# An attention and MLP kernel: the first chunk's squared scores stored unturned and turned where four later chunks read them

## Chip, cores and metric

The kernel runs on one core of one Trainium2 chip. The metric is the device time of one execution in microseconds (us). Every time below is of that kind or a time within one profiled execution.

## What is computed

For two samples (`batch` 2), with S = 3136 tokens, D = 256 features and 64 query features, the reference does three stages, one behind the other:

```python
scores = scale * np.matmul(z, z.transpose(0, 2, 1))   # scale = 1 / S
attn = np.maximum(scores, 0.0) ** 2
out = np.matmul(attn, v)
x = u * out
```

Then come `_moe_ref` (a rank 32 token mixing `x^T U V` and a channel MLP of 256 to 1024 to 256 with a ReLU) and `_moe2_ref` (the real part of an FFT over tokens and features, a normalisation and a second channel MLP). The change is in the first stage alone. Its matrix `attn` is symmetric, since queries and keys are both z.

## The kernel before, in words

**Tiles and steps.** Each sample b is cut into 7 chunks of CH = 448 queries; a chunk is written (b, qc). The keys are cut into 12 pairs of two times 128 keys, and a short pair 12 of 64 keys. One step is a chunk and a pair. A step makes a tile `A` of 128 x 896, keys on partitions, two halves of 448 queries in the row, with the squared scores, and splits it into a rounded high part `h` and the rest `l`. `values` then runs 24 matmuls with both (`psO`, line 780).

**Three ways to get `A`.** `scores` (lines 697 to 758) computes it: 6 matmuls on PE (`psS`, line 724), Relu and Square on ACT (lines 744 and 745), the cast to `h` on ACT or DVE (line 750 or 751, shown as L135 where ACT does it through the helper `hcopy`), and the subtraction `l` on DVE (helper `sub`, L138). Or the tile is a *kept* one: a chunk further back has already made these scores as seen from the other side, `keep` (lines 680 to 705) turned them on DVE in blocks of 32 x 32 (L690, L687 for pair 12) and stored them to DRAM (`kept_d`, L700, on the queues of POOL and SP), and `load_kept` (L671, on ACT's queue) reads them back; `split_kept` then only casts (ACT) and subtracts (DVE). What a chunk stores where is said by `_stored` and `_target`.

**What is kept.** `_kept` gives the pairs that chunk (b, qc) reads: all pairs that end before the chunk begins, but for sample 0 not the pairs 0 and 1, whose keys belong to the first chunk (pair 1 to the first and the second). The first chunk of sample 0 stores nothing. Pairs 0 and 1 of sample 0 have their keys in plain order (`_plain`): the first chunk of all takes its keys straight from its queries; everywhere else a pair's two halves are its even and its odd keys.

**What sets the order.** `_pairs` writes out the order of the 13 steps of each chunk: the steps of the kept pairs at given places, the others between them. The loop calls `ahead(i + 2)` and then `values(i)`, so scores or split of a step are issued two steps before its values. `ahead` also starts the load of a kept step three steps ahead (line 936), carries out the stores that the step before prepared, and drives background work: input loads, and converters of weights (L215 to L223 on DVE, L218 and L219 on ACT, tiles `stg`). PE, DVE, ACT and POOL carry out their instructions in the order in which they are issued; SP issues DMAs only.

**Buffers.** `P` (computed tiles) has 4, `h` and `l` have 3 each, `turned` (turned and loaded tiles) 5, `psS` 2.

Of the kernel before, what the change touches and what calls it, by code (L numbers as in the profile page):

```python
# [21 lines left out]
CH = 448  # L22
# [20 lines left out]

def _plain(b, p):
    return (b == 0) & (p < 2)


def _kept(b, qc):

    return [p for p in range(12) if 256 * (p + 1) <= qc * CH and (b or 256 * p >= CH)]  # L50

# [14 lines left out]
def _pairs(b, qc):  # L66

    plain = [*range(6), 12, *range(6, 12)]
    if qc == 0:
        return plain  # L70
    kept = _kept(b, qc)
    made = [p for p in range(12) if p not in kept]
    heavy = [p for p in made if _stored(b, qc, p)]
    bare = [p for p in made if p not in heavy]

    def merged(x, y):
        at = [((k + 0.5) / len(z), n, v) for n, z in enumerate((x, y)) for k, v in enumerate(z)]
        return [v for _, _, v in sorted(at)]

    places = sorted([12, 7, 8, 3, 10, 5, 4, 9, 2, 11][: len(kept)])  # L80
    short = 1 if len(kept) == 10 else 6
    places = [n for n in range(3, 13)] if short == 1 else places
    order = dict(zip(places, kept)) | {short: 12}
    rest = [n for n in range(13) if n not in order]
    order.update(zip(rest, bare[:2] + merged(bare[2:], heavy)))
    return [order[n] for n in range(13)]
# [38 lines left out]
def program(ctx, tc, zT, v, uT, U, V, w1a, w2a, w1b, w2b, b49, f64, fd, rep, mask, out):  # L125
# [28 lines left out]
    def run(gen):  # L154
# [13 lines left out]
        if _kept(b, c)  # L168
    }
    V_d = dram.tile([2 * RANK, S], F32R, tag="Vd", name="Vd")  # L170
    e_d = dram.tile([NB, 57 * 64], F32, tag="ed", name="ed")
# [316 lines left out]
    def attention(stack):  # L488
# [16 lines left out]
        def load_z(b, i, pairs=slice(0, 3)):  # L505

            raw = turned_tile()
            for j, r in enumerate(halves):
                if i < 4:
                    dma = late_dma if i == 0 or j and i > 1 else load  # L510
                    t0, n = 768 * i + 256 * pairs.start, pairs.stop - pairs.start
                    if _plain(b, 3 * i + pairs.start):
                        src = zT[b, :, t0 : t0 + 256 * n].rearrange("d (p j n) -> d j p n", j=2, n=128)
                        dma(out=raw[r, 0 : 128 * n].rearrange("d (p n) -> d p n", n=128), in_=src[:, j])
                    else:
                        dma(out=raw[r, 0 : 256 * n], in_=zT[b, :, t0 + j : t0 + j + 256 * n])
                else:
                    (late_dma if j else load)(out=raw[r, 0:64], in_=zT[b, :, S - 64 : S])
            zraw[b, i] = raw
# [24 lines left out]
        def split_z(b, i, pairs=slice(0, 3)):  # L544
# [3 lines left out]
            if i < 4:  # L548
                h, l = (KT[b][:, 3 * i : 3 * i + 3, k][:, pairs] for k in range(2))
                n = pairs.stop - pairs.start  # L550
                if _plain(b, 3 * i + pairs.start):
                    raw = raw[:, 0 : 128 * n].rearrange("d (p n) -> d p n", n=128)
                else:
                    raw = raw[:, 0 : 256 * n].rearrange("d (p n w) -> d p n w", n=128, w=2)[:, :, :, 0]
                (nc.vector.tensor_copy if (b, pairs.start) == (0, 2) else hcopy)(h, raw)
                sub(l, raw, f(h))
                return
# [28 lines left out]
        def load_v(b, p):  # L586
# [5 lines left out]
            if p < 12:  # L592
                how = "(a p) n -> p a n" if _plain(b, p) else "(p a) n -> p a n"
                load(out=raw, in_=v[b, p * 256 : p * 256 + 256, :].rearrange(how, a=2))
            else:
# [67 lines left out]

        prob, kept, loads, writes, turns = {}, {}, [None, None], [], []

        def load_kept(b, qc, p):
            own = next((k for k in range(2) if loads[k] not in kept), None)
            A = kept[b, qc, p] = ptile() if own is None else turned_tile()
            if own is not None:
                loads[own] = b, qc, p  # L670
            nc.scalar.dma_start(out=c2(A), in_=kept_d[b, qc][256 * p : 256 * p + 256].rearrange("(m j) n -> m j n", j=2))  # L671

# [8 lines left out]
        def keep():  # L681
# [13 lines left out]
            def write():  # L695
                for k, (a, to, col) in enumerate(_stored(b, qc, p)):
                    t0, t1 = max(rows.start, 0 if b else 512), min(rows.stop, 256 * (to * CH // 256))
                    m0, m1 = (n * (x - rows.start) // 32 for x in (t0, t1))
# [5 lines left out]

            writes.append(write)

        def scores(b, qc, p):
# [5 lines left out]
            for kk, kq in ((0, 0), (0, 1), (1, 0)):  # L713
                for j, r in enumerate(halves):
                    if p == 12:
                        k = KTl[b][r, kk]
                    elif (b, qc) == (0, 0) and p < 2:
                        c = 256 * p + 128 * j
                        k = q[r, kk, c : c + 128]
                    else:  # L720
# [4 lines left out]
                    elif (kk, kq) == (0, 0):  # L725
                        dst = extra if j else ps[:, j]
                        mm(dst[:, 0:w], first_q[r, c : c + 128], first_q[r, 0:w], start=True, stop=True)
            A, h, l = ptile(), ctile("h", F32R), ctile("l", F32R)
# [13 lines left out]
            else:  # L742
# [13 lines left out]
                if stored:  # L756
                    turns.append((b, qc, p, A))
            prob[b, qc, p] = (h, l)

# [165 lines left out]
        def ahead(i):  # L925
            if i < len(steps):
# [7 lines left out]
                elif i:  # L934
                    scores(b, qc, p)
                if i + 3 < len(steps) and steps[i + 3][2] in _kept(*steps[i + 3][0:2]):
                    load_kept(*steps[i + 3])
                for write in done:
# [484 lines left out]
```

## Time and profile before

| what | value |
|---|---|
| median of 3 runs | 1084.86 us (1084.63 to 1085.54) |
| the profiled execution's own time | 1084.36 us |
| span of that execution in the trace | 1082.6 us |
| granted clock of TensorE (1.00 is full speed) | 1.00 |
| PE, DVE, ACT, POOL busy, share of the span | 99%, 78%, 58%, 24% |
| chunk (0,2), first to last values | 82.90 to 119.88 us |
| chunk (0,3) | 119.88 to 155.26 us |
| chunk (0,4) | 155.26 to 189.27 us |
| chunk (0,5) | 189.27 to 222.92 us |

A chunk's stretch goes from the first matmul of its values to the first of the next chunk's. PE is the matmul engine, PEld its weight loads, DVE the vector engine, ACT the scalar engine, SP and POOL the engines whose queues carry most DMAs. The views used are the page's parts, the groups of instructions by line and shape, the engines by stretch, the chain of waits, and the timelines of one engine. In the view by stretch below, the five rows are the chunks (0,2) to (0,5) and the chunk (1,2) of the other sample; behind each engine's busy time stands its count of instructions in brackets.

### The profile page before, as it was taken

The numbers are of one execution on the slowest core, as the hardware profiler recorded it, in microseconds if no ns is written. First come the engines' busy times: TensorE is split into PE (matmuls) and PEld (weight loads), VectorE is DVE, ScalarE is ACT, GpSimd is POOL, SyncE is SP. The second block draws the span as 40 slices with busy tenths as digits, with TensorE's granted clock in tenths as the row PEclk, the third lists the DMA queues.
The fourth block names the chain that finished last, engine by engine and source line by source line (L and its number), as shares of the span: only waits on it lengthen the run. The fifth ranks groups of instructions, "written<-read, shape, count | busy, mean of one in ns | idle before, by whom it ended". The sixth has DMA issues, their size and how long they took to land.

```text
span 1082.6 us, 21193 instructions
## 1 busy us (share of the span) xinstructions
PE 1075.2 (99%) x7926; PEld 1005.4 (93%) x7926; DVE 848.0 (78%) x1571; ACT 623.8 (58%) x1094; POOL 255.5 (24%) x426
## 2 busy tenths in 40 slices
PE   9999999999999999999999999999999999999998
PEld 7999999999999999989899999999999999999997
DVE  7898888988998988656667876676687888778863
ACT  7888777768888877543333534343355454444431
POOL 2133345222343344121101121211131111011100
PEclk9999999999999999999999999999999999999999
DMA  6256567784666677785532553321253221121210
GB/s 178 78 145 174 162 190 223 231 273 117 185 193 195 192 239 221 264 259 175 156 89 71 155 158 101 79 75 40 66 132 96 61 91 44 35 67 45 60 43 35
DMA packets 140519, 146.04 MB, mean 135 GB/s; under 512 B 72534, under 2 KB 113530, under 8 KB 140416
## 3 DMA queue, kind: packets, MB, share of 16 engines
q1 hardware_dynamic: 108704, 70.57, 22.7%
q0 software_dynamic: 23280, 47.72, 15.3%
q10 hardware_dynamic: 8432, 26.40, 7.6%
q8 instruction: 62, 1.02, 0.4%
q14 instruction: 41, 0.34, 0.1%
HBM read 88.61 MB, written 56.00 MB: 134 GB/s over the span
## 4 chain that ended last, share of the span: by engine, by line
PE 95%; ACT 2%; DMA 1%; DVE 1%; issue 0%; SPq 0%; ACTq 0%; DVEq 0%
PE psO L780 37%; PE psC L460 8%; PE psC L459 8%; PE psC L458 8%; PE psH L435 8%; PE psH L433 8%; PE psH L434 8%; PE psS L724 6%; DMA scr<-wst 0%; ACT P L744 0%; DMA vraw<-in_v 0%; PE ps_m L1183 0%; ACT P L745 0%; PE ps_g L1183 0%; PE ps_x L1183 0%
## 5 line engine op out<-in xcount | busy, mean ns | idle before, releaser
L780 PE MATMUL psO<-h,Vt 64*128 64x448 f32 x2744 | 321.3, 360 | 0.5 <-DVE h L751 0.2
L780 PEld LDWEIGHTS psO<-h,Vt 64*128 64x128 f32 x2744 | 267.8, 184 | 16.3 <-DVE h L751 1.9
L438 ACT ACTIVATE Hh<-psH 128x448 fp32r<-128x448 f32 x224 | 121.4, 543 | 245.0 <-PE psH L435 243.6
L439 DVE SCALAR_TENSOR_TENSOR Hl<-psH,Hh 128x448 fp32r<-128x448 f32 x224 | 138.1, 619 | 111.0 <-ACT Hh L438 109.1
L138 DVE TENSOR_TENSOR l<-P,h 128x896 fp32r<-128x896 f32 (+2 forms) x188 | 170.6, 914 | 50.1 <-ACT h L135 43.2
L780 PE MATMUL psO<-l,Vt 64*128 64x448 f32 x1372 | 183.2, 359 | 0.1
L433 PE MATMUL psH<-h,w 128*128 128x448 f32 x448 | 165.1, 368 | 0.0
L435 PE MATMUL psH<-h,w 128*128 128x448 f32 x448 | 162.6, 363 | 0.0
L460 PE MATMUL psC<-Hh,w 128*128 128x448 f32 x448 | 162.5, 363 | 0.0
L434 PE MATMUL psH<-l,w 128*128 128x448 f32 x448 | 162.4, 363 | 0.0
L459 PE MATMUL psC<-Hl,w 128*128 128x448 f32 x448 | 162.3, 362 | 0.0
L458 PE MATMUL psC<-Hh,w 128*128 128x448 f32 x448 | 162.1, 362 | 0.0
L700 POOL DMA_DIRECT2D kept<-turned x178 | 112.9, 640 | 155.6 <-DVE turned L690 106.7
L780 PEld LDWEIGHTS psO<-l,Vt 64*128 64x128 f32 x1372 | 138.5, 184 | 7.8 <-DVE l L138 1.0
L744 ACT ACTIVATE P<-psS 128x896 f32<-128x896 f32 (+1 forms) x124 | 107.9, 870 | 22.7 <-PE psS L724 21.3
L745 ACT ACTIVATE P<-P 128x896 f32<-128x896 f32 (+1 forms) x124 | 113.1, 912 | 3.9
L135 ACT CAST h<-P 128x448 fp32r<-128x448 f32 (+1 forms) x111 | 80.2, 733 | 57.7 <-DVE P L324 39.6
L433 PEld LDWEIGHTS psH<-h,w 128*128 128x128 f32 x448 | 84.2, 188 | 6.3 <-issue 0.3
L459 PEld LDWEIGHTS psC<-Hl,w 128*128 128x128 f32 x448 | 84.0, 188 | 6.2 <-DVE Hl L439 0.4
L434 PEld LDWEIGHTS psH<-l,w 128*128 128x128 f32 x448 | 84.2, 188 | 5.6
L458 PEld LDWEIGHTS psC<-Hh,w 128*128 128x128 f32 x448 | 84.0, 188 | 5.9 <-issue 0.2
L460 PEld LDWEIGHTS psC<-Hh,w 128*128 128x128 f32 x448 | 84.1, 188 | 5.3
(299 smaller groups left out, 1359.3 us busy)
## 6 DMA issues: line engine op xcount, KB each, us to landing
turned<-kept ACTq DMA_DIRECT2D x49, 448.0 KB, 4.0
kept<-turned POOLq DMA_DIRECT2D x102, 112.0 KB, 3.6
uT<-in_uT SPq DMA_DIRECT2D x14, 448.0 KB, 5.7
out<-P SPq DMA_DIRECT2D x27, 224.0 KB, 1.9
aTd<-turned POOLq DMA_DIRECT2D x13, 448.0 KB, 4.1
kept<-turned SPq DMA_DIRECT2D x51, 112.0 KB, 2.9
aNd<-turned POOLq DMA_DIRECT2D x40, 112.0 KB, 3.7
scr<-wst SPq DMA_DIRECT2D x16, 256.0 KB, 2.0
```

What stands on the lines that cost most here:

```text
L138: tt(out=o, in0=a, in1=b, op=ALU.subtract)
L433: mm(ps[:, 0:CH], wh, self.h[:, a], start=a == 0, stop=False)
L434: mm(ps[:, 0:CH], wh, self.l[:, a], start=False, stop=False)
L435: mm(ps[:, 0:CH], wl, self.h[:, a], start=False, stop=a == 1)
L438: act(out=h, in_=ps[:, 0:CH], func=AF.Relu)
L439: stt(out=l, in0=ps[:, 0:CH], scalar=0.0, in1=f(h), op0=ALU.max, op1=ALU.subtract)
L458: mm(dst, wh, h, start=k == 0, stop=False)
L459: mm(dst, wh, l, start=False, stop=False)
L460: mm(dst, wl, h, start=False, stop=k == 7)
L700: (load if k % 2 and qc < 3 else late_dma)(out=kept_d[b, to][t0:t1, col : col + n].rearrange("(b r) k -> r b k", r=32), in_=t[quads[a], m0 ...
L745: act(out=A[:, x], in_=A[:, x], func=AF.Square)
L780: mm(o[fa][i][:, 0:CH], vt[r, j, k, fa * 128 : fa * 128 + 128], x[r, j * CH : j * CH + CH], start=n0 == 0 and fa not in [t[1][0] for t in ...
```

## The change

Chunk (0,0) writes the squared scores of pairs 3 to 10 to a DRAM tile `first_d` as they are, eight writes of 448 KB on POOL's queue. The chunks (0,2) to (0,5) (`LATE`) now have pairs 0 and 1 among their kept ones. Their tiles are read on SP's queue, four steps ahead: for pair 0 four pieces of 32 partitions from `first_d`, for pair 1 three pieces from `first_d` and one, already turned, from `kept_d`. One step before the split, `turn_read` turns the pieces on DVE (L692 of the new file) into a `P` tile. The plain layout goes away; the first chunk now takes every other query as keys. The stored rows for those chunks begin at 448 in place of 512. `_pairs` sets new places:

| chunk | pairs in order, before | pairs in order, after |
|---|---|---|
| (0,2) | 0 1 5 6 3 7 12 8 9 4 10 11 2 | 3 4 5 6 7 0 12 8 1 9 10 11 2 |
| (0,3) | 0 1 7 5 8 9 12 2 3 10 6 11 4 | 5 6 7 2 8 9 12 0 3 10 1 11 4 |
| (0,4) | 0 1 8 2 9 7 12 3 4 10 5 11 6 | 7 8 9 2 3 0 12 4 1 10 5 11 6 |
| (0,5) | 0 1 8 2 10 3 12 4 5 9 6 11 7 | 8 9 10 2 3 0 12 4 1 5 6 11 7 |

Kept before were pair 2 in (0,2), pairs 2 to 4 in (0,3), 2 to 6 in (0,4) and 2 to 7 in (0,5); pairs 0 and 1 join them. The core of the diff:

```diff
+LATE = (2, 3, 4, 5)
+
+def _unturned(b, qc, p):
+    return b == 0 and qc in LATE and p < 2
...
-    return [p for p in range(12) if 256 * (p + 1) <= qc * CH and (b or 256 * p >= CH)]
+    return [p for p in range(12) if 256 * (p + 1) <= qc * CH and (b or 256 * p >= CH or qc in LATE)]
...
     places = sorted([12, 7, 8, 3, 10, 5, 4, 9, 2, 11][: len(kept)])
+    if _unturned(b, qc, 0):
+        others, at = kept[2:], {3: (0, 1), 5: (1, 3)}.get(len(kept), (2, 4))
+        for p, k in enumerate(at):
+            others.insert(k, p)
+        places = [5, 8, 12] if len(kept) == 3 else places
+        kept = others
...
+    first_d = dram.tile([S, CH], F32, tag="firstd", name="firstd")
...
-            nc.scalar.dma_start(out=c2(A), in_=kept_d[b, qc][256 * p : 256 * p + 256].rearrange("(m j) n -> m j n", j=2))
+            rows = slice(256 * p, 256 * p + 256)
+            if not _unturned(b, qc, p):
+                nc.scalar.dma_start(out=c2(A), in_=kept_d[b, qc][rows].rearrange("(m j) n -> m j n", j=2))
+                return
+            n = (CH - rows.start) // 64 if p else 4
+            src = first_d[qc * CH : qc * CH + CH, rows.start : rows.start + 64 * n].rearrange("(b s) (q c) -> q s b c", s=32, c=64)
+            for q in range(n):
+                load(out=A[quads[q]].rearrange("s (b c) -> s b c", c=64), in_=src[q])
+            B = None
+            if n < 4:
+                B = ptile()
+                load(
+                    out=c2(B)[quads[3]], in_=kept_d[b, qc][rows][64 * n :].rearrange("(m j) n -> m j n", j=2)
+                )
+            unturned[b, qc, p] = B, slice(0, 32 * n)
+
+        def turn_read(b, qc, p):
+            B, r = unturned.pop((b, qc, p))
+            B = ptile() if B is None else B
+            nc.vector.transpose(
+                out=B[r].rearrange("p (j b s) -> p j b s", j=2, s=32),
+                in_=kept[b, qc, p][r].rearrange("p (b c j) -> p j b c", j=2, c=32),
+            )
+            kept[b, qc, p] = B
...
                     elif (b, qc) == (0, 0) and p < 2:
-                        c = 256 * p + 128 * j
-                        k = q[r, kk, c : c + 128]
+                        k = dealt(q[r, kk, 256 * p : 256 * p + 256], j)
...
+                if b + qc == 0 and 256 * (p + 1) > LATE[0] * CH and 256 * p < (LATE[-1] + 1) * CH:
+                    dst = first_d[256 * p : 256 * p + 256].rearrange("(m j) n -> m j n", j=2)
+                    writes.append(lambda: late_dma(out=dst, in_=c2(A)))
...
-                if i + 3 < len(steps) and steps[i + 3][2] in _kept(*steps[i + 3][0:2]):
-                    load_kept(*steps[i + 3])
+                for s in steps[i + 3 : i + 5]:
+                    if s[2] in _kept(*s[0:2]) and _unturned(*s) == (s != steps[i + 3]):
+                        load_kept(*s)
+                if steps[i + 1 : i + 2] and steps[i + 1] in unturned:
+                    turn_read(*steps[i + 1])
```

Line numbers of the new file: `hcopy` L144, `sub` L147, the converters L225 to L233, the new turn L692, `keep` L715 and L712, Relu and Square L771 and L772, DVE's cast L778. Where instructions stand now is shown at three places.

DVE in chunk (0,2), from the `keep` turn behind step 3 on; steps 4 to 7 (pairs 3, 7, 12, 8 before; 7, 0, 12, 8 now). Before:

```order
L690 STREAM_TRANSPOSE turned<-P 128x14x2x32
L751 CAST h<-P 128x896
L138 TENSOR_TENSOR l<-P,h 128x896 x2
L215 TENSOR_SCALAR stg<-stg 128x192
L216 TENSOR_SCALAR stg<-stg 128x192
L138 TENSOR_TENSOR l<-P,h 64x448
L690 STREAM_TRANSPOSE turned<-P 128x14x2x32
L687 STREAM_TRANSPOSE turned<-P 64x448
L751 CAST h<-P 128x896
L138 TENSOR_TENSOR l<-P,h 128x896
```

Now:

```order
L715 STREAM_TRANSPOSE turned<-P 128x14x2x32
L147 TENSOR_TENSOR l<-P,h 128x896
L692 STREAM_TRANSPOSE P<-turned 128x896
L147 TENSOR_TENSOR l<-P,h 128x896
L715 STREAM_TRANSPOSE turned<-P 128x14x2x32
L225 TENSOR_SCALAR stg<-stg 128x192
L226 TENSOR_SCALAR stg<-stg 128x192
L147 TENSOR_TENSOR l<-P,h 64x448
L712 STREAM_TRANSPOSE turned<-P 64x448
L778 CAST h<-P 128x896
L147 TENSOR_TENSOR l<-P,h 128x896
L692 STREAM_TRANSPOSE P<-turned 96x896
```

The cast of step 4 has gone to ACT, the turn of step 5 (L692) stands in front of that step's subtraction, and a second turn, of step 8, stands behind the subtraction of step 7.

ACT in chunk (0,2), from the Relu of step 7 to the Square or cast of step 9; `Us` is a converter's output. Before:

```order
L744 ACTIVATE P<-psS 128x896
L745 ACTIVATE P<-P 128x896
L744 ACTIVATE P<-psS 128x896
L745 ACTIVATE P<-P 128x896
L135 CAST h<-P 128x896
L135 CAST Q<-qraw 128x448
L135 COPY Us<-stg 128x192
L744 ACTIVATE P<-psS 128x896
L745 ACTIVATE P<-P 128x896
L671 DMA turned<-kept_76 128x896
```

Now:

```order
L771 ACTIVATE P<-psS 128x896
L772 ACTIVATE P<-P 128x896
L144 CAST h<-P 128x896
L144 CAST Q<-qraw 128x448
L144 COPY Us<-stg 128x192
L771 ACTIVATE P<-psS 128x896
L772 ACTIVATE P<-P 128x896
L144 CAST h<-P 128x896
```

Step 8 is now a cast alone, of the tile that DVE turned, ahead of the Q cast, the copy and the Relu of step 9.

DVE in chunk (0,4), from the subtraction of pair 12 (step 6) on; steps 7 and 8 are pairs 3 and 4 before, 4 and 1 now. Before:

```order
L138 TENSOR_TENSOR l<-P,h 64x448
L138 TENSOR_TENSOR l<-turned,h 128x896
L687 STREAM_TRANSPOSE turned<-P 64x448
L221 SCALAR_TENSOR_TENSOR stg<-stg 128x196
L222 SCALAR_TENSOR_TENSOR stg<-stg 128x196
L223 TENSOR_TENSOR stg<-stg 128x196
L138 TENSOR_TENSOR l<-turned,h 128x896
```

Now:

```order
L147 TENSOR_TENSOR l<-P,h 64x448
L147 TENSOR_TENSOR l<-turned,h 128x896
L712 STREAM_TRANSPOSE turned<-P 64x448
L692 STREAM_TRANSPOSE P<-turned 96x896
L231 SCALAR_TENSOR_TENSOR stg<-stg 128x196
L232 SCALAR_TENSOR_TENSOR stg<-stg 128x196
L233 TENSOR_TENSOR stg<-stg 128x196
L147 TENSOR_TENSOR l<-P,h 128x896
```

The new turn of pair 1 stands between the turn of pair 12 for `keep` and a converter's three steps, ahead of the subtraction of step 8.

## Rows read from the trace of the kernel before

**Rows 1.** The page, part 1, busy time, share of the span, instructions of each engine.
```profile
PE 1075.2 (99%) x7926; PEld 1005.4 (93%) x7926; DVE 848.0 (78%) x1571; ACT 623.8 (58%) x1094; POOL 255.5 (24%) x426
```

**Rows 2.** The page, part 4, the chain that ended last, shares by engine.
```profile
PE 95%; ACT 2%; DMA 1%; DVE 1%; issue 0%; SPq 0%; ACTq 0%; DVEq 0%
```

**Rows 3.** Stretch, length, busy PE PEld DVE ACT POOL, clock, DMA share, GB/s.
```profile
82.90:119.88 36.98, 36.86 (x368) 33.86 (x366) 32.26 (x47) 30.04 (x41) 11.84 (x18) 1.00 0.57 158
119.88:155.26 35.38, 35.38 (x356) 32.80 (x354) 30.27 (x49) 27.49 (x40) 18.08 (x29) 1.00 0.64 188
155.26:189.27 34.01, 34.01 (x344) 32.35 (x342) 29.45 (x49) 27.61 (x41) 15.58 (x25) 1.00 0.74 218
189.27:222.92 33.65, 33.65 (x340) 32.67 (x338) 29.88 (x50) 25.11 (x40) 8.37 (x13) 1.00 0.69 223
328.85:364.30 35.45, 35.45 (x359) 34.79 (x356) 32.55 (x49) 30.18 (x42) 11.57 (x18) 1.00 0.71 198
```

**Rows 4.** The chain of waits inside (0,4): start, length, what.
```profile
171.98 0.60 PE psS L724 x6
172.58 4.80 PE psO L780 x48
```

**Rows 5.** Groups by line and shape, DVE, 82.9 to 222.92 us, the four chunks.
```profile
L138 DVE TENSOR_TENSOR l<-P,h 128x896 fp32r<-128x896 f32 x33 | 36.0, 1092 | 8.2 <-ACT h L135 6.4
L690 DVE STREAM_TRANSPOSE turned<-P 128x896 f32<-128x896 f32 x18 | 19.9, 1104 | 0.1
...
L751 DVE CAST h<-P 128x896 fp32r<-128x896 f32 x21 | 13.0, 619 | 2.3 <-ACT P L745 2.3
```

**Rows 6.** The same view, ACT.
```profile
L745 ACT ACTIVATE P<-P 128x896 f32<-128x896 f32 x33 | 31.5, 955 | 1.0
L744 ACT ACTIVATE P<-psS 128x896 f32<-128x896 f32 x34 | 31.0, 912 | 4.8 <-PE psS L724 4.4
...
L135 ACT CAST h<-P 128x896 fp32r<-128x896 f32 x12 | 11.3, 945 | 0.4
```

**Rows 7.** The timeline of DVE in (0,2), start, length, instruction.
```profile
92.86 1.11 DVE L690 STREAM_TRANSPOSE turned<-P 128x896 f32<-128x896 f32 x1
...
101.55 0.35 DVE L221 SCALAR_TENSOR_TENSOR stg<-stg 128x192 int32<-128x192 int32 x1
...
102.49 1.11 DVE L690 STREAM_TRANSPOSE turned<-P 128x896 f32<-128x896 f32 x1
```

**Rows 8.** The timeline of DVE in (0,4).
```profile
171.40 1.09 DVE L138 TENSOR_TENSOR l<-turned,h 128x896 fp32r<-128x896 f32 x1 [0.51 <-PE psO L780]
172.41 0.63 DVE L687 STREAM_TRANSPOSE turned<-P 64x448 f32<-64x448 f32 x1
```

**Rows 9.** The timeline of ACT in (0,2).
```profile
90.47 0.95 ACT L745 ACTIVATE P<-P 128x896 f32<-128x896 f32 x1
...
102.81 0.94 ACT L135 CAST h<-P 128x896 fp32r<-128x896 f32 x1
...
104.38 0.91 ACT L744 ACTIVATE P<-psS 128x896 f32<-128x896 f32 x1
...
106.18 0.44 ACT L218 ACTIVATE stg<-stg,maskc 128x192 int32<-128x192 uint16 x1
...
106.87 0.90 ACT L744 ACTIVATE P<-psS 128x896 f32<-128x896 f32 x1
```

**Rows 10.** The timeline of PE in (0,2).
```profile
101.87 1.76 PE L780 MATMUL psO<-h,Vt 64*128 64x448 f32 x16
...
113.37 1.07 PE L780 MATMUL psO<-h,Vt 64*128 64x448 f32 x8
```

**Rows 11.** The timeline of ACT in (0,4).
```profile
172.11 0.56 ACT L135 CAST Q<-qraw 128x448 fp32r<-128x448 f32 x1
...
174.25 0.91 ACT L744 ACTIVATE P<-psS 128x896 f32<-128x896 f32 x1
...
176.18 0.95 ACT L135 CAST h<-P 128x896 fp32r<-128x896 f32 x1
```

**Rows 12.** The timeline of PE in (0,4).
```profile
177.82 1.77 PE L780 MATMUL psO<-h,Vt 64*128 64x448 f32 x16
```

**Rows 13.** DMA issues of the whole run: count, KB each, median us to landing.
```profile
turned<-kept ACTq DMA_DIRECT2D x49, 448.0 KB, 4.0
...
kept<-turned SPq DMA_DIRECT2D x51, 112.0 KB, 2.9
```

More of the change, by code (lines that the diff above doesn't have):

```diff
@@ L41, in _orders @@
     return o1, o2, c1, c2, tok, feat
-def _plain(b, p):
-    return (b == 0) & (p < 2)
+LATE = (2, 3, 4, 5)
+def _unturned(b, qc, p):
+    return b == 0 and qc in LATE and p < 2
 def _kept(b, qc):
-    return [p for p in range(12) if 256 * (p + 1) <= qc * CH and (b or 256 * p >= CH)]
+    return [p for p in range(12) if 256 * (p + 1) <= qc * CH and (b or 256 * p >= CH or qc in LATE)]
 def _target(p, a):
@@ L511, in load_z @@
                     t0, n = 768 * i + 256 * pairs.start, pairs.stop - pairs.start
[L512 to L516, printed above, removed]
+                    dma(out=raw[r, 0 : 256 * n], in_=zT[b, :, t0 + j : t0 + j + 256 * n])
                 else:
@@ L550, in split_z @@
                 n = pairs.stop - pairs.start
[L551 to L554, printed above, removed]
+                raw = raw[:, 0 : 256 * n].rearrange("d (p n w) -> d p n w", n=128, w=2)[:, :, :, 0]
                 (nc.vector.tensor_copy if (b, pairs.start) == (0, 2) else hcopy)(h, raw)
@@ L592, in load_v @@
             if p < 12:
-                how = "(a p) n -> p a n" if _plain(b, p) else "(p a) n -> p a n"
-                load(out=raw, in_=v[b, p * 256 : p * 256 + 256, :].rearrange(how, a=2))
+                load(out=raw, in_=v[b, p * 256 : p * 256 + 256, :].rearrange("(p a) n -> p a n", a=2))
             else:
@@ L662, in conversions @@
                 yield conv_w(w2a, k, True, wa[1])
-        prob, kept, loads, writes, turns = {}, {}, [None, None], [], []
+        prob, kept, loads, writes, turns, unturned = {}, {}, [None, None], [], [], {}
         def load_kept(b, qc, p):
@@ L696, in write @@
                 for k, (a, to, col) in enumerate(_stored(b, qc, p)):
-                    t0, t1 = max(rows.start, 0 if b else 512), min(rows.stop, 256 * (to * CH // 256))
+                    t0, t1 = max(rows.start, 0 if b else CH if to in LATE else 512), min(rows.stop, 256 * (to * CH // 256))
                     m0, m1 = (n * (x - rows.start) // 32 for x in (t0, t1))
@@ L705, in keep, with dealt @@
             writes.append(write)
+        def dealt(x, j):
+            return x.rearrange("d (n w) -> d n w", w=2)[:, :, j]
         def scores(b, qc, p):
@@ L726, in scores @@
                         dst = extra if j else ps[:, j]
-                        mm(dst[:, 0:w], first_q[r, c : c + 128], first_q[r, 0:w], start=True, stop=True)
+                        mm(dst[:, 0:w], dealt(first_q[r, 0:256], j), first_q[r, 0:w], start=True, stop=True)
             A, h, l = ptile(), ctile("h", F32R), ctile("l", F32R)
```

## Prediction

> **What bounds the kernel now.** The page's first line is read first: the matmul engine PE is busy 99% of the span, DVE 78%, ACT 58% [rows 1]. The chain that ended last is 95% PE [rows 2]. So a matmul that goes away is worth its full time, unless something else then makes PE wait. Next the stretches of the four chunks that change, (0,2) to (0,5): PE is busy 36.86 of 36.98 us in (0,2) and all of the time in the others, but DVE is busy 32.26, 30.27, 29.45 and 29.88 us, 87%, 86%, 87% and 89% of its stretches, far above its mean over the kernel, and ACT 75% to 81% [rows 3]. Both take their instructions in order, so a wait on either passes to all that stands behind it. What a step costs PE is seen in the chain of a stretch: 0.60 us for six score matmuls, 4.80 us for two steps of values, 2.40 each [rows 4].
>
> **What the change removes.** Eight score steps (pairs 0 and 1 in four chunks): 8 x 0.60 = 4.8 us of PE. This is the gain if no wait appears. ACT loses a Relu of 0.912 and a Square of 0.955 per step [rows 6]; of the casts some move from DVE (0.619 [rows 5]) to ACT (0.945 [rows 6]), as a kept step is always cast on ACT. ACT so gains at least 0.92 us per step.
>
> **What it adds on DVE.** A turn of 128x896 per step, priced by the turn of the same shape that `keep` makes: 1.104 us [rows 5]. Where a DVE cast of 0.619 goes, the net is 0.49; eight times that is 3.9 us, in chunks where DVE has only 3.8 to 5.1 us of idle time each [rows 3]. That alone fits. What counts is the place: the turn stands on DVE behind the subtraction of the step before (and often behind a `keep` turn), and ACT's cast of the turned step stands in front of the next Relu in ACT's queue. Before, ACT started such a step from PSUM alone. Now ACT must wait for DVE, and the next computed step waits behind that.
>
> **The walk through (0,2).** Step n's values are v(n). Pair 0 is step 5, pair 1 step 8. On DVE a `keep` turn starts at 92.86 [rows 7]. Behind it stand the subtraction of step 4 (1.09, its successor 1.0 later, as 171.40 to 172.41 [rows 8]), then the new turn (1.03 the same way): it ends near 96.0. ACT has finished step 4's Square at 91.42 [rows 9], casts until 92.4 and then stands until 96.0. Its cast of step 5 ends near 96.95. On DVE follow subtraction and `keep` (2.05), the converters' two short steps; ACT, with its own two converter steps (0.7, as 106.18 to 106.87 [rows 9]) in between, reaches Relu of step 7 only near 100.05, its Square ends near 101.95, and DVE's cast (0.6) at 102.5. PE began v(7) at 101.87 [rows 10] and is now ready 1.2 earlier, at 100.67: it waits about 1.85. Then subtraction, second turn and cast of step 8 end at 105.6, where PE is ready at 105.5: 0.1. Behind that cast stand the Q cast and a copy, so Relu of step 9 starts near 106.3 instead of 104.38 [rows 9]. ACT had no idle time from 102.81 on in this stretch, and has none now: Relu, Square and cast of step 9 end at 109.1 (PE ready 108.6, wait 0.5), those of step 10 at 112.6 (ready 111.5, wait 1.1), and DVE's cast of step 11, behind a conversion (0.94, as 101.55 to 102.49 [rows 7]) and a `keep`, at 116.25 (ready 115.6, wait 0.65). v(11) began at 113.37 [rows 10]. The waits are 4.2, less 1.2 for two score steps: **+3.0 us**.
>
> **The walk through (0,4).** Pair 1 is step 8, right behind pair 12, step 6. The subtraction of step 7 began at 171.40 [rows 8]; DVE has a turn in place of a cast ahead of it (+0.49), and 0.51 idle there; I take half, 171.65. Then `keep` of pair 12 (from 172.65, 0.56), then the new turn, 173.2 to 174.3. ACT's cast of step 8 then runs from 174.3 to 175.25; before, the Q cast behind it began at 172.11 [rows 11]. Q, key and converter casts (about 1.1) follow, and Relu of step 9 starts at 176.3 instead of 174.25, 2.05 later. Its cast began at 176.18 and ended at 177.13 [rows 11]; now it ends near 179.2. v(9) began at 177.82 [rows 12] and cannot start before 179.2, so the chunk loses **1.4 us**, though PE could be ready at 177.82 - 1.2 = 176.6.
>
> **The other two.** In (0,3) the turned steps are 7 and 10, with computed steps 9 and 11 behind them as in (0,4): I take the same **+1.4**. In (0,5) the step after the second turned one is a kept one, so the casts on ACT delay no Relu: the last wait of (0,4), by which PE ready at 178.3 behind a v(8) that starts at 175.3 stands until 179.2, falls away. 1.4 - 0.9 = **+0.5**. Sum: 3.0 + 1.4 + 1.4 + 0.5 = +6.3 us.
>
> **Loads, writes and layout.** The reads from the first chunk's scores go on SP, in 112 KB pieces of 256-byte rows, four per step, four steps ahead; the turn is one step ahead, so at least 3 x 2.40 = 7.2 us remain. The nearest row is the write of the same size and row length on the same queue, 2.9 us to landing, and a 448 KB read of long rows takes 4.0 [rows 13]. Bounds: 2.9 if the four overlap, 11.6 if they follow one another. I take 4 to 5, nearest the 448 KB read, so hidden: nothing. On SP input loads queue behind them; they are issued steps ahead too. The Trainium skill, "DMA: Bandwidth & Descriptors", section "Specifications", speaks against such rows: it asks for at least 512 bytes for line rate, and says that below this the engine reads, modifies and writes. By it the estimate would be twice the long-row read, 8.0 us, so 0.8 late where the lead is 7.2; the write's 2.9 us for rows of 256 bytes speaks against that as far as writes show it. The eight 448 KB writes of the first chunk go on POOL behind no one's critical load but the late keys of that chunk: nothing, at most half of a 4.0 us transfer, 2.0, if keys come late. The strided weight loads of the first chunk are 14; with a mean load of 1005.4/7926 = 0.127 us [rows 1], a doubling in plain sight would be 1.8; I take nothing, as PE hides loads under the matmul before. V of pairs 0 and 1 now comes in one longer row: nothing, or a gain of some tenths.
>
> **Sum.** The profiled execution took 1084.36 us; the median of the runs is 1084.86, 0.5 above it. 1084.36 + 6.3 + 0.5 = 1091.2 us.
>
> **Rivals.** *The waits are absorbed, faster.* Sample 1's chunks have the same number of kept steps, already turned; (1,2) takes 35.45 us with DVE busy 92% and PE 100% [rows 3], 1.53 less than (0,2). So a full DVE alone does not stop PE. If the turns land in DVE's gaps, or PE's queue is further ahead than I reckon, the kernel gets the 4.8: 1084.36 - 4.8 + 0.5 = 1080.1, up to 1082.5 with 2.4 of waits left. It decides for this when waits sum to less than 2.6 us of the 11.1 I find. Against it: in (0,2) Relu of step 9 has no ACT idle time behind it to be caught up in. Chance 0.27. *Gain and waits cancel*, each wait about half of what I walked: 5.6 less 4.8 is +0.8, 1085.7, and 1082.5 to 1087 around it. Chance 0.12. *The SP reads come late*, because they follow one another on the queue or stand behind a stalled input load: DVE, in order, then stands at the turn with all its work. Landing 0.8 us after DVE gets there, at each of the eight places, adds 6.4 to the forecast: 1097.6. Chance 0.08; it is outside the range. By the Trainium skill's rule above, this would be the case to expect. *The change does not do what it says*: that PE makes the eight steps anyway is excluded by its order, which drops 48 matmuls; no chance of its own.
>
> **How the numbers follow.** My forecast, waits of the size walked, has 0.53 and its own range 1087 to 1094: the lower end two thirds of the waits (7.4 - 4.8 + 1084.86), the upper one the walk plus the 2.0 of late keys and some tenths. Its place is 1091.2. The range 1080.1 to 1094.0 takes in both other cases and leaves out the late reads and the edges. About 0.2% (2.2 us) is what a measurement of this kernel can tell from no change: faster by more 0.27, within 0.12, slower by more 0.08 + 0.53 = 0.61.
>
> **What would show it.** Right: PE busy less by about 4.8 us but the span longer; in (0,2) and (0,4) the chain leaves PE for DVE turns and ACT casts; ACT idle time before casts of turned steps, ended by the new DVE turn; (0,2) near 40 us, (0,5) near 34. Wrong: chunks shorter by 1.2 us each with PE 99% busy or more in them (waits absorbed), or DVE idle before the new turns, ended by a DMA of the first chunk's scores (late reads), or the first chunk longer (layout or late keys).

## The result and the profile after

The changed kernel takes 1092.14 us (median of 6 runs, 1091.07 to 1094.77), the kernel before 1085.05 us beside it (1084.50 to 1085.63). The ratio is 1.0068 with an interval of 1.0055 to 1.0081: slower by about 7.1 us, where 1091.2 us, slower by 6.3, was forecast.

Two lines of the changed kernel's page (span 1091.3 us): busy time of each engine, and the chain's shares by engine.

```profile
PE 1075.1 (99%) x7878; PEld 1001.6 (92%) x7878; DVE 851.2 (78%) x1571; ACT 616.1 (56%) x1086; POOL 260.9 (24%) x434
...
PE 88%; ACT 4%; DVE 3%; DMA 3%; issue 2%; SPq 1%; ACTq 0%; DVEq 0%; POOL 0%
```

PE makes 48 matmuls fewer than before (7878 against 7926 [rows 1]), the eight score steps. Yet its busy time has not changed, 1075.1 against 1075.2 us. The chain, 95% PE before [rows 2], is now 88% PE, with ACT 4% and DVE 3%.

The four chunks of the changed kernel by stretch, from the first values of the chunk to those of the next; columns as in [rows 3].

```profile
82.91:122.92 40.01, 37.09 (x357) 33.10 (x354) 33.34 (x47) 28.09 (x39) 11.57 (x18) 1.00 0.65 177
122.92:161.01 38.09, 35.35 (x344) 31.38 (x342) 31.07 (x49) 25.74 (x38) 17.11 (x28) 1.00 0.70 196
161.01:196.53 35.52, 34.37 (x332) 30.38 (x330) 30.44 (x49) 25.78 (x39) 15.87 (x26) 1.00 0.77 226
196.53:231.73 35.20, 33.07 (x326) 30.99 (x325) 30.54 (x50) 23.25 (x38) 8.01 (x13) 1.00 0.77 238
```

| chunk | before, us | after, us | measured | forecast |
|---|---|---|---|---|
| (0,2) | 36.98 | 40.01 | +3.03 | +3.0 |
| (0,3) | 35.38 | 38.09 | +2.71 | +1.4 |
| (0,4) | 34.01 | 35.52 | +1.51 | +1.4 |
| (0,5) | 33.65 | 35.20 | +1.55 | +0.5 |
| sum | 140.02 | 148.82 | +8.80 | +6.3 |

The span is 8.7 us longer (1091.3 against 1082.6), so all of the loss lies in these four chunks. The profiled execution took 1093.06 us, 0.9 above its kernel's median, and that of before 0.7 below; the medians differ by 7.1. Since 4.8 us of score matmuls went away, the four chunks hold 8.80 + 4.8 = 13.6 us of new waits.

Where PE waits in (0,2) of the changed kernel: the first matmul rows of v(3), v(7), v(9), v(10) and v(11), with PE's idle time before each and what ended it.

```profile
91.82 1.88 PE L810 MATMUL psO<-h,Vt 64*128 64x448 f32 x16 [0.34 <-DVE h L778]
...
102.63 1.87 PE L810 MATMUL psO<-h,Vt 64*128 64x448 f32 x16 [1.16 <-DVE h L778]
...
109.36 1.87 PE L810 MATMUL psO<-h,Vt 64*128 64x448 f32 x16 [0.21 <-ACT h L144]
...
112.82 1.88 PE L810 MATMUL psO<-h,Vt 64*128 64x448 f32 x16 [0.78 <-ACT h L144]
...
116.41 0.88 PE L810 MATMUL psO<-h,Vt 64*128 64x448 f32 x6 [0.30 <-DVE h L778]
```

Before, v(7) and v(11) began at 101.87 and 113.37 [rows 10]. What holds PE is the high part `h`, cast on ACT or DVE. ACT's timeline in the same stretch, its casts of the two turned steps (5 and 8) and the Relu of step 9:

```profile
96.07 0.94 ACT L144 CAST h<-P 128x896 fp32r<-128x896 f32 x1 [3.65 <-DVE P L692]
...
104.87 0.94 ACT L144 CAST h<-P 128x896 fp32r<-128x896 f32 x1 [2.95 <-DVE P L692]
...
106.44 0.91 ACT L771 ACTIVATE P<-psS 128x896 f32<-128x896 f32 x1
```

ACT stands 3.65 and 2.95 us for the new turn, L692. Behind the second wait Relu of step 9 starts at 106.44, where it started at 104.38 [rows 9].

Who waited for whom in these chunks (total us, times, longest):

```profile
ACT h L144 <- DVE P L692: 18.7, 6, 3.8
...
PE psO L810 <- ACT h L144: 6.4, 8, 1.8
```

The new turn itself never waited. The larger of its two groups in the view by line (count, busy us, mean ns, idle us before them); the other, of three, shows 0.0 us of idle time too:

```profile
L692 DVE STREAM_TRANSPOSE P<-turned 96x896 f32<-96x896 f32 (+1 forms) x5 | 5.4, 1086 | 0.0
```

So no read came late for a turn in this execution.

### The profile page after: what moved, and what is told of

Its sections match the earlier page's. It is cut to its first block, busy times and chain, and to the rows that moved or that the text cites. A ratio compares the mean times of both kernels' runs of the same rounds, so it can differ in the third digit from the quotient of the medians.

```text
span 1091.3 us, 21164 instructions
## 1 busy us (share of the span) xinstructions
PE 1075.1 (99%) x7878; PEld 1001.6 (92%) x7878; DVE 851.2 (78%) x1571; ACT 616.1 (56%) x1086; POOL 260.9 (24%) x434
## 4 chain that ended last, share of the span: by engine, by line
PE 88%; ACT 4%; DVE 3%; DMA 3%; issue 2%; SPq 1%; ACTq 0%; DVEq 0%; POOL 0%
PE psO L810 29%; PE psH L445 8%; PE psH L443 8%; PE psC L470 8%; PE psH L444 8%; PE psC L469 8%; PE psC L468 8%; PE psS L751 5%; ACT P L772 1%; ACT P L771 1%; ACT h L144 1%; DMA kept<-turned 1%; DVE l L147 1%; DVE turned L715 1%; DMA vraw<-in_v 0%
## 5 line engine op out<-in xcount | busy, mean ns | idle before, releaser
L147 DVE TENSOR_TENSOR l<-P,h 128x896 fp32r<-128x896 f32 (+2 forms) x189 | 171.7, 914 | 54.7 <-ACT h L144 48.2
L144 ACT CAST h<-P 128x896 fp32r<-128x896 f32 (+1 forms) x120 | 88.7, 748 | 76.5 <-DVE P L334 39.6
L771 ACT ACTIVATE P<-psS 128x896 f32<-128x896 f32 (+1 forms) x116 | 100.7, 868 | 19.0 <-PE psS L751 17.8
L772 ACT ACTIVATE P<-P 128x896 f32<-128x896 f32 (+1 forms) x116 | 105.5, 909 | 3.7
L443 PEld LDWEIGHTS psH<-h,w 128*128 128x128 f32 x448 | 84.1, 188 | 6.3 <-issue 0.3
L468 PEld LDWEIGHTS psC<-Hh,w 128*128 128x128 f32 x448 | 83.9, 187 | 5.8 <-issue 0.2
L445 PEld LDWEIGHTS psH<-h,w 128*128 128x128 f32 x448 | 84.0, 188 | 5.2
```

The source lines that it names most:

```text
L147: tt(out=o, in0=a, in1=b, op=ALU.subtract)
L443: mm(ps[:, 0:CH], wh, self.h[:, a], start=a == 0, stop=False)
L445: mm(ps[:, 0:CH], wl, self.h[:, a], start=False, stop=a == 1)
L468: mm(dst, wh, h, start=k == 0, stop=False)
L772: act(out=A[:, x], in_=A[:, x], func=AF.Square)
```

## The experiments

The forecast's theory: what costs is the place of the turn in DVE's order, which makes ACT and then PE late. Rival 1: DVE is too full in these chunks, wherever the turn stands. Rival 2: the reads on SP are late or hold up other transfers. All ratios are against the kernel before, run beside each. Each edit is shown against the changed kernel unless another is named, and a line of three dots marks lines left out.

**The turn in front of the step before it.**

```diff
+                if steps[i + 1 : i + 2] and steps[i + 1] in unturned:
+                    turn_read(*steps[i + 1])
                 if (b, qc, p) in kept:
                     split_kept(b, qc, p)
...
-                if steps[i + 1 : i + 2] and steps[i + 1] in unturned:
-                    turn_read(*steps[i + 1])
```

> The changed kernel, but each new DVE turn is issued before the split or scores of the step in front of it, not behind them: the same work, the turn stands ahead of the earlier step's subtraction and keep turn. Theory (the loss is the place: ACT's cast of a turned step waits for DVE and holds up the Relu behind it): the waits at the casts mostly go, 1081 to 1086 us. Rival 1 (DVE is simply too full in these chunks): the same DVE time, so 1090 to 1093. Rival 2 (the reads on SP are late or hold up other loads): the turn wants its data a step sooner, so 1092 or more, with DVE idle before the turns.

Measured: 1085.02 us, ratio 1.0004 (0.9995 to 1.0014). The four chunks:

```profile
85.28:122.67 37.39, 36.52 (x356) 32.49 (x354) 33.11 (x47) 28.18 (x39) 11.65 (x18) 1.00 0.70 190
122.67:156.83 34.16, 34.16 (x344) 31.94 (x342) 30.85 (x49) 25.72 (x38) 17.14 (x28) 1.00 0.80 217
156.83:191.19 34.36, 34.16 (x332) 30.56 (x330) 30.29 (x49) 25.97 (x39) 15.81 (x26) 1.00 0.79 233
191.19:224.74 33.55, 32.95 (x326) 30.22 (x324) 30.40 (x50) 23.43 (x38) 7.98 (x13) 1.00 0.79 246
```

and ACT's waits for the turn in them:

```profile
ACT h L144 <- DVE P L692: 6.6, 4, 2.1
```

The same eight turns, moved by one place, take the four chunks from 148.82 to 139.46 us. Rival 1 in its plain form is out: DVE's busy time there is 124.65 us, as against 125.39. Rival 2 is out as the main cause: the turns want their data a step sooner and the kernel is faster. (0,3) is 1.22 us shorter than before, the full price of its two score steps; (0,2) and (0,4) are still 0.41 and 0.35 longer.

**The cast of the turned steps on DVE.**

```diff
-            hcopy(h, A)
+            (nc.vector.tensor_copy if _unturned(b, qc, p) else hcopy)(h, A)
```

> The changed kernel, but the high part of the eight turned steps is cast on DVE right behind the turn (0.62 us) instead of on ACT (0.94 us). ACT has nothing to wait for at these steps. Theory (ACT standing behind DVE): Relu of the next computed step starts in time, 1083 to 1088 us. Rival 1 (DVE too full): 8 x 0.62 = 5.0 us more on DVE, so 1094 to 1097. Rival 2 (SP): unchanged, 1091 to 1093.

Measured: 1095.18 us, 1.0091 (1.0076 to 1.0107): slower still, a miss for the theory as it was put there, and inside the 1094 to 1097 us that rival 1 gave. ACT's timeline in (0,2) shows why:

```profile
99.03 0.46 ACT L228 ACTIVATE stg<-stg,maskc 128x192 int32<-128x192 uint16 x1 [2.48 <-DVE stg L225]
...
105.42 0.35 ACT L144 COPY Us<-stg 128x192 f32<-128x192 f32 x1 [3.35 <-DVE stg L233]
105.68 0.91 ACT L771 ACTIVATE P<-psS 128x896 f32<-128x896 f32 x1
```

ACT no longer waits at the cast, but at the converters: L228 reads what DVE made in L225, the copy to `Us` what it made in L233, and both stand on DVE behind the turn. Relu of step 9 starts at 105.68, 0.8 earlier than with the cast on ACT and still 1.3 later than before. So the cast is only one of the links by which DVE's lateness reaches ACT. The first three chunks are 0.2 to 0.3 us shorter than in the changed kernel (39.73, 37.77, 35.29), the fourth is 2.4 longer (37.64); the last section says what happened there. So rival 1 gave the time but not what made it: in the first three chunks DVE is busy for 1.0 to 1.4 us more, and they got shorter.

**No turn at all.** The kernel leaves out the eight turns and uses the tiles as they were read.

```diff
-                B = ptile()
                 load(
-                    out=c2(B)[quads[3]], in_=kept_d[b, qc][rows][64 * n :].rearrange("(m j) n -> m j n", j=2)
+                    out=c2(A)[quads[3]], in_=kept_d[b, qc][rows][64 * n :].rearrange("(m j) n -> m j n", j=2)
                 )
-            unturned[b, qc, p] = B, slice(0, 32 * n)
...
-                if steps[i + 1 : i + 2] and steps[i + 1] in unturned:
-                    turn_read(*steps[i + 1])
```

> The changed kernel without the eight DVE turns: the tiles that SP read are split as they came, so the squared scores of pairs 0 and 1 in chunks (0,2) to (0,5) are used unturned. All reads, casts and buffers stay. Theory and rival 1 (turn in the wrong place, or too much DVE work): the gain of the eight score steps comes through, 1080 to 1082 us. Rival 2 (SP reads): most of the loss stays, 1087 or more.

Measured: 1082.76 us, 0.9987 (0.9975 to 1.0000). The four chunks:

```profile
82.80:119.23 36.43, 35.98 (x356) 33.05 (x354) 31.13 (x45) 28.10 (x39) 11.53 (x18) 1.00 0.73 196
119.23:153.38 34.15, 34.15 (x344) 31.63 (x342) 28.81 (x47) 25.61 (x38) 17.14 (x28) 1.00 0.77 211
153.38:187.00 33.62, 33.52 (x334) 30.45 (x331) 28.36 (x47) 26.09 (x39) 15.82 (x26) 1.00 0.84 245
187.00:221.10 34.10, 32.42 (x327) 29.97 (x324) 28.35 (x48) 23.37 (x38) 7.98 (x13) 1.00 0.78 244
```

138.30 us: 10.5 of the 13.6 us of waits go with the turns. The bulk agrees with the theory and with rival 1, which this run does not tell apart, and not with rival 2. The edit takes away more than DVE's work, though: the `P` tiles that the turns filled are no longer taken, where the expectation says that all buffers stay, and this run does not tell DVE's work from the buffers. 3.1 us of waits stay, 1.65 of them in (0,5), and there they are one wait, of ACT for the last 64 keys (`KTl`) and of PE for ACT:

```profile
205.29 0.39 ACT L144 CAST KTl<-vraw 128x64 fp32r<-128x64 f32 x2 [3.29 <-DMA vraw<-in_zT]
```

```profile
206.57 1.88 PE L808 MATMUL psO<-h,Vt 64*128 64x448 f32 x16 [1.68 <-ACT h L144]
```

v(7) began at 202.33, so v(8) could have begun 2.40 us later, at 204.73; it began 1.8 us behind that. In this place rival 2 holds: a transfer is late that stands on SP behind the reads, as the fifth run shows. What stays in (0,2) and (0,4), 0.65 and 0.81 us, was not followed up.

**The layout alone.**

```diff
-LATE = (2, 3, 4, 5)
+LATE = ()
...
-                if b + qc == 0 and 256 * (p + 1) > LATE[0] * CH and 256 * p < (LATE[-1] + 1) * CH:
+                if LATE and b + qc == 0 and 256 * (p + 1) > LATE[0] * CH and 256 * p < (LATE[-1] + 1) * CH:
```

> The kernel before with only the change of layout: pairs 0 and 1 of sample 0 dealt into even and odd keys, the first chunk taking every other query as keys; nothing is stored unturned and pairs 0 and 1 are computed in every chunk in the old order. Theory and both rivals: 1084.5 to 1085.6 us, no cost. If the layout or the strided weight loads cost: 1086 to 1087.

Measured: 1085.48 us, 1.0009 (0.9997 to 1.0022), no difference that can be told. The dealt keys and the strided weight loads cost nothing that shows within that interval.

**The reads behind the other loads of their step.** In `ahead`, `load_kept` of an unturned tile moves from before the step's stores to behind `load_keys`.

```diff
-                for s in steps[i + 3 : i + 5]:
-                    if s[2] in _kept(*s[0:2]) and _unturned(*s) == (s != steps[i + 3]):
-                        load_kept(*s)
+                s = steps[i + 3] if i + 3 < len(steps) else None
+                if s and s[2] in _kept(*s[0:2]) and not _unturned(*s):
+                    load_kept(*s)
...
                     load_keys(since // 2)
+                s = steps[i + 4] if i + 4 < len(steps) else None
+                if s and s[2] in _kept(*s[0:2]) and _unturned(*s):
+                    load_kept(*s)
```

What it is aimed at, in the changed kernel: SP's issues in (0,5), and ACT's two casts of the last 64 keys ahead of the cast of step 8.

```profile
204.37 1.89 SPq L680 DMA_DIRECT2D turned<-firstd  x3
...
210.10 1.11 SPq L574 DMA_DIRECT2D qraw<-in_zT  x2
211.33 1.16 SPq L533 DMA_DIRECT2D vraw<-in_zT  x2
```

```profile
215.92 0.39 ACT L144 CAST KTl<-vraw 128x64 fp32r<-128x64 f32 x2 [3.22 <-DMA vraw<-in_zT]
```

The reads of pair 1 begin at 204.37 and the load of the last keys stands on SP behind them until 211.33; ACT, in order, waits 3.22 us for it and casts step 8 only at 216.22. Between the two stands the load of the next queries (`qraw`), which itself waited 3.2 us until 210.10; what for was not tried. The edit moves the reads behind both loads.

> The changed kernel with one thing moved: in each step the reads of the unturned tiles are issued on SP behind that step's stores and loads of queries and keys, not in front of them, so a read that waits for its buffer no longer holds up the key load of 64 keys in (0,5). Theory (place of the turn; SP adds the last bit): (0,5) gets 0.8 us shorter, as ACT's wait of 3.2 us for those keys goes, the waits behind the turns stay: 1091 to 1092 us. Rival (SP is the cause of most of the loss): 1086 or less.

Measured: 1092.63 us, 1.0070 (1.0055 to 1.0085). (0,2) and (0,5):

```profile
83.21:123.23 40.02, 37.07 (x357) 33.33 (x355) 33.34 (x47) 28.10 (x39) 11.54 (x18) 1.00 0.67 182
...
196.75:231.17 34.42, 33.07 (x327) 30.00 (x324) 30.28 (x50) 23.24 (x38) 7.98 (x13) 1.00 0.76 241
```

(0,5) is 0.78 shorter than in the changed kernel, (0,2) unchanged. The time of the whole kernel does not show the 0.78 (1092.63 against 1092.14 for the changed kernel). The run was also to settle a doubt that the chain of waits raised. Inside (0,2) the changed kernel's chain runs through SP: reads, then a store of a `turned` tile (95.23 to 98.06), then the `keep` turn, L715, that wants its buffer. But with the reads last the chain still runs through that store, so this run does not settle it. DVE's rows of the changed kernel do:

```profile
97.04 1.09 DVE L147 TENSOR_TENSOR l<-P,h 128x896 fp32r<-128x896 f32 x1 [1.06 <-ACT h L144]
98.05 1.10 DVE L715 STREAM_TRANSPOSE turned<-P 128x896 f32<-128x896 f32 x1
```

The turn starts 1.01 us behind the subtraction and without idle time, as the turn of step 8 does at 103.69 behind a subtraction at 102.68. So it did not wait for the store; the path through SP only ties with the one through DVE.

**Both moves together.** The edits of the first and the fifth run.

> Both edits together: each turn ahead of the work of the step in front of it, and the reads behind the other loads of their step. Theory: the loss by place is gone and the key wait in (0,5) too, the four chunks together 139 us or less: 1083 to 1085 us. Rival (the reads now land too late for a turn that is a step sooner): 1086 or more, DVE idle before turns.

Measured: 1088.19 us, 1.0033 (1.0020 to 1.0046): a miss, the rival's case by its time. The first three chunks are as with the turn first alone (37.41, 34.17, 34.45); (0,5) takes 35.90 instead of 33.55. A wait of PE early in the chunk and DVE's turn of pair 1 there:

```profile
195.49 1.87 PE L810 MATMUL psO<-h,Vt 64*128 64x448 f32 x16 [1.29 <-DVE h L778]
```

```profile
207.15 1.11 DVE L692 STREAM_TRANSPOSE P<-turned 96x896 f32<-96x896 f32 x1 [0.98 <-DMA turned<-firstd]
```

The turn now stands 0.98 us for its read: issued later and wanted earlier, the read has lost its lead. But the early wait, of 1.29 us for a cast on DVE, is the larger, and why it came was not followed up. In the next run, with the same two moves, the turn still stands 0.68 us for its read and (0,5) takes 33.67, so the late read alone does not make the 35.90.

**Fewer converters in (0,2) and (0,4).** The edit to the run with both moves:

```diff
-            (0, 1): (2, 8), (0, 2): (2, 5, 9), (0, 3): (2, 5, 9), (0, 4): (2, 5, 9), (0, 5): (2, 5),
-            (1, 0): (3, 9), (1, 1): (2, 9), (1, 2): (2, 5, 9), (1, 3): (2, 5, 9), (1, 4): (2, 5),
+            (0, 1): (2, 5, 8), (0, 2): (2, 9), (0, 3): (2, 5, 9), (0, 4): (2, 9), (0, 5): (2, 5),
+            (1, 0): (3, 6, 9), (1, 1): (2, 5, 9), (1, 2): (2, 5, 9), (1, 3): (2, 5, 9), (1, 4): (2,),
```

> As the run before it, and the converters' start points thinned out: (0,2) and (0,4) start two each in place of three, (0,1), (1,0) and (1,1) one more each, (1,4) one less; the same 25 conversions. If what is left of the waits in (0,2) and (0,4) comes from DVE being full there, and from ACT being tied to DVE by the converters: these two chunks lose 0.5 to 1 us each, 1081.5 to 1084 us. If not: as the run before, within 0.5 us.

Measured: 1088.21 us, 1.0025 (1.0016 to 1.0034), a miss for the time. The chunks (0,2) and (0,5):

```profile
84.48:120.54 36.06, 35.96 (x358) 33.28 (x356) 32.09 (x43) 27.25 (x36) 11.65 (x18) 1.00 0.74 198
...
188.56:222.23 33.67, 32.95 (x327) 29.98 (x324) 30.14 (x50) 23.38 (x38) 7.98 (x13) 1.00 0.76 238
```

(0,2) gets 1.35 us shorter than in the run before it and (0,4), at 33.86, 0.59, as the theory has it: without one converter they run below the kernel before (36.98 and 34.01). But the chunks that took the converters over pay more: (0,1), at 37.84, takes 0.89 us more than the 36.95 of the kernel before; (1,0) and (1,1), at 38.28 and 39.02, take 1.33 and 2.17 more than their 36.95 and 36.85. (1,4), which gave one up, also took 34.44 instead of 32.75; why was not looked into. A converter is work for DVE and for ACT; which of the two makes it cost was not tried.

**Only (0,3) and (0,5), turn first, reads last.**

> Turn first and reads last, but only chunks (0,3) and (0,5) use pairs 0 and 1 kept; (0,2) and (0,4) compute them in the old order. In the run with the turn first (0,3) was 1.2 us shorter than before, (0,2) and (0,4) 0.4 longer. If a chunk's gain hangs on its own order alone: (0,2) and (0,4) as before, (0,3) 1.2 and (0,5) 0.5 to 1 shorter, 1082.5 to 1084 us. If the chunks hang together (buffers, queues): no faster than the run with all four.

Its edit to the run with both moves is `LATE = (3, 5)`. Measured: 1087.42 us, 1.0022 (1.0010 to 1.0034). (0,2), (0,3) and (0,4) came out as expected, 36.97, 34.16 and 33.95 us; (0,5) took 35.28, here because its turn stands for its read:

```profile
205.51 1.11 DVE L692 STREAM_TRANSPOSE P<-turned 96x896 f32<-96x896 f32 x1 [2.28 <-DMA turned<-firstd]
```

**Only (0,3), turn first.** The first run's kernel with `LATE = (3,)`.

> Turn first, reads in their old place, and only chunk (0,3) uses pairs 0 and 1 kept. In the run with the turn first for all four, (0,3) was 1.2 us shorter than before, its two score steps in full. If that hangs on the order inside the chunk: (0,3) at 34.2 us, all other chunks as before, 1083.7 us, 0.1% under the kernel before. If it was lent by the other chunks: 1085 or more.

Measured: 1084.09 us, 0.9990 (0.9981 to 0.9999). The chunk (0,3):

```profile
120.00:154.15 34.15, 34.15 (x345) 31.61 (x342) 30.85 (x49) 25.69 (x38) 17.79 (x29) 1.00 0.76 208
```

1.23 us shorter than before, the other three as before (37.00, 33.95, 33.64): the gain hangs on the order inside the chunk.

**(0,3) and (0,5), turn first, the last keys loaded one step earlier.** The first run's kernel with `LATE = (3, 5)` and

```diff
-                if since in range(0, 13, 2):
-                    load_keys(since // 2)
+                if since in (0, 2, 4, 6, 8, 10, 11):
+                    load_keys((since + 1) // 2)
```

> Turn first, reads in their old place, chunks (0,3) and (0,5), and the load of the last 64 keys of sample 1 issued one step earlier, so that it stands ahead of the read of pair 1 on SP. If the key load behind a read that waits for its buffer is what holds (0,5) at 33.55 us with the turn first: (0,3) 34.2, (0,5) 32.6 to 33.0, 1082.9 to 1083.4 us. If something else does: (0,5) 33.5 or more, 1083.6 or more.

Measured: 1083.46 us, 0.9988 (0.9978 to 0.9997), the best of the kernels that make all the turns, faster than the kernel before by about 1.3 us of 1085. (0,3) and (0,5):

```profile
119.81:153.97 34.16, 34.16 (x346) 31.96 (x343) 30.89 (x49) 25.61 (x38) 17.31 (x28) 1.00 0.75 207
...
187.91:220.97 33.06, 32.71 (x327) 30.94 (x325) 30.35 (x50) 23.30 (x38) 8.28 (x13) 1.00 0.79 251
```

Both gain, (0,5) by 0.59 us, a little less than expected. ACT no longer waits at the cast of the last keys, where with the turn first in all four chunks it still stood 1.68 us; so the key load behind the reads was at least part of what was left in (0,5). No run has these two chunks without the earlier key load, so its share is not shown alone. The idea of the change is worth something where its waits are taken out.

## Why the prediction was right, and where a term was not

**The walk through (0,2) held from v(7) on.** Forecast against measured starts: v(7) 102.5 and 102.63, Relu of step 9 106.3 and 106.44, v(9) 109.1 and 109.36, v(10) 112.6 and 112.82, v(11) 116.25 and 116.41. Durations of the trace before, put in the new order, were enough. One thing ahead of v(7) it had wrong: PE was not ready there 1.2 us earlier than before, but 0.6. With the score step of pair 0 gone, v(3) could have begun at 91.31, where the row ahead of it makes room, and waited for DVE's cast until 91.82 (91.91 before), so the first 0.6 us was lost at once. The wait before v(7) was 1.36 us (101.27 to 102.63) and not 1.85. The sum is the same, since DVE's cast and not PE sets when v(7) starts. The first run shows the mechanism: the turn in another place, all else kept, and the loss is gone.

**The walk through (0,4) held in its path.** The chunk begins 161.01 - 155.26 = 5.75 us later than before. DVE's turn of step 8, ACT's Relu of step 9 and PE's v(9):

```profile
178.65 1.06 DVE L692 STREAM_TRANSPOSE P<-turned 96x896 f32<-96x896 f32 x1
```

```profile
181.69 0.91 ACT L771 ACTIVATE P<-psS 128x896 f32<-128x896 f32 x1
```

```profile
184.60 1.88 PE L810 MATMUL psO<-h,Vt 64*128 64x448 f32 x16 [0.54 <-ACT h L144]
```

Less 5.75 these are 172.90, 175.94 and 178.85; forecast were 173.2, 176.3 and 179.2. So v(9) was 1.03 us later than before and not 1.4. The chunk lost 1.51 all the same, as 0.12 came in v(9) and 0.36 in the last two steps, which the walk did not have. That the sum is so near is in part luck.

**The term that failed is "the other two".** (0,3) was set equal to (0,4) and lost 2.71 instead of 1.4. Its first turned step, pair 0 as step 7, is not like one of (0,4): DVE's turn and ACT's cast of it were

```profile
139.80 1.11 DVE L692 STREAM_TRANSPOSE P<-turned 128x896 f32<-128x896 f32 x1
```

```profile
141.00 0.94 ACT L144 CAST h<-P 128x896 fp32r<-128x896 f32 x1 [2.33 <-DVE P L692]
```

```profile
141.99 1.87 PE L810 MATMUL psO<-h,Vt 64*128 64x448 f32 x16 [1.75 <-ACT h L144]
```

Before, ACT's cast of step 7, of a kept tile, began at 136.07; now it waits 2.33 us for the turn and begins at 141.00, 4.93 later, of which 3.04 is the chunk's later start. DVE's row ahead of the turn is a full `keep` turn at 138.65, 1.11 us, where in (0,4) it is pair 12's of 0.63. v(7) begins 19.07 us into the chunk, against 17.75 before (137.63 - 119.88): 1.32 of the 2.71 is lost there, and 1.39 behind it, where the second turned step stands. So the +1.4 fits the second turned step, the one that the walk through (0,4) had followed; the first was priced at nothing. This is read from the rows and was not tried alone; a walk of its own would have shown the wait. (0,5) lost 1.55 instead of 0.5; 0.78 of that is the key load behind the reads, by the fifth run; without turns that load makes PE wait 1.8 us. "Hidden: nothing" for the loads that queue behind the reads on SP was the wrong step: the reads were in time, what stood behind them was not.

**The total came nearer than its parts.** Forecast were 1091.2 us and measured 1092.14, 0.9 apart; the four chunks lost 8.80 and not 6.3, 2.5 apart. The forecast added 0.5 because the median before lay above the profiled execution, and the changed kernel's median lies 0.9 below its own. That this made up for a part of the 2.5 is luck.

**The reads.** Their median time to landing in the changed kernel (count, KB each, us):

```profile
P<-firstd SPq DMA_DIRECT2D x11, 112.0 KB, 3.7
```

The view has a time for these 11 of the 28 pieces; with the reads last the other 17 have a median of 3.7 too. 3.7 us for a 112 KB piece with three others beside it, against 4.0 for a 448 KB read in long rows [rows 13]. The prediction's estimate of 8.0 us for rows of 256 bytes, worked out from the rule in the Trainium skill ("DMA: Bandwidth & Descriptors", section "Specifications"), is not what these reads took; no turn of the changed kernel waited for one.

**The sign that was wrong.** PE's busy time was to fall by 4.8 us. It did not move, though 48 matmuls went: in the four chunks 8.93 us show as idle and some 4.7 of the 13.6 us of waits count as busy. A matmul's row runs on into a wait behind it (v(3) waited 0.51 us, of which 0.34 show), and the first row behind a wait is longer: 1.71 us from 102.63 to the next at 104.34, where v(7) before takes 1.60. Length of stretches tells such waits; busy time does not. Of the other signs, ACT's idle time before the turned casts and (0,2) near 40 us came; (0,5), named as near 34, took 35.20.

**The rivals.** "The waits are absorbed" was out: its best case, 1080.1, was not even reached without any turn (1082.76). "Gain and waits cancel" needed 5.6 us of waits; the chunks held 13.6. "The reads come late" did not happen in the changed kernel, and happened at once when their lead was cut. The layout cost nothing that shows, as taken.

## What to carry to other kernels

When engines take work in order, price an added instruction by who stands behind it, through every link: walk the queues with measured durations, for each place anew, and not by analogy from one place to the next. Compare a forecast with the result part by part, since a total can agree while its parts do not. An instruction whose input is ready early belongs ahead of the older step's work, not behind it; that moved 7 us here at no cost in work. On a queue of transfers, ask of a read that waits for its buffer what is queued behind it.

## What the runs showed of the hardware

In two executions time in which PE stood was followed by a lower granted clock, so that it cost more than its length. With the cast on DVE, PE stood 2.16 us in (0,5) before step 8, and the next step's values began 4.70 us later, at 221.87, instead of 3.0 (2.40 and a score step):

```profile
217.17 3.15 PE L810 MATMUL psO<-h,Vt 64*128 64x448 f32 x16 [2.16 <-DVE h L700]
```

The granted clock in stretches of 2 us there is the third number from the right. PE was busy for 1.01 and 0.83 of 2.00 us; then the clock was 0.50, 1.2 instead of 2.4 GHz.

```profile
214.00:216.00 2.00, 1.01 (x12) 0.60 (x8) 1.86 (x5) 0.86 (x3) 1.19 (x2) 1.00 0.98 329
216.00:218.00 2.00, 0.83 (x6) 0.75 (x8) 1.86 (x4) 1.25 (x2) 0.00 (x0) 0.86 1.03 387
218.00:220.00 2.00, 2.00 (x14) 1.79 (x12) 2.00 (x6) 0.58 (x2) 0.00 (x0) 0.50 0.86 278
```

The same was seen at the start of the profiled execution with the turn first. PE was idle for 1.14 us in 4 to 8 us and for 0.46 in 8 to 10, and had the half clock in the next stretch; its first chunk took 38.99 instead of 37.60 us. That execution took 1086.81 us where its kernel's median is 1085.02, so kernels that differ by 1 us were compared here by stretches and by medians, not by one execution.

```profile
8.00:10.00 2.00, 1.54 (x12) 0.98 (x14) 1.57 (x4) 1.97 (x5) 0.00 (x0) 1.00 0.97 244
10.00:12.00 2.00, 2.00 (x14) 1.79 (x12) 1.75 (x4) 1.97 (x4) 0.00 (x0) 0.51 0.72 236
```

In the changed kernel PE's waits, of up to 1.77 us shown as idle, left the clock at 1.00 in all four chunks; in its stretch from 216 to 218 us PE was busy for only 0.79 us and kept it. So the length of one wait does not tell whether the clock falls, and that the waits made it fall is not shown.
